# Gathering the second expert's rows ahead of its weights, with shorter index arithmetic, in a three-stage kernel

## The chip, the cores and the metric

The kernel runs on one core of one Trainium2 chip. The metric is the device time of one execution in microseconds (us). A core has TensorE (matmuls; PE in the profile, PEld for its weight loads), VectorE (DVE), ScalarE (ACT), GpSimd (POOL) and SyncE (SP), which work side by side and wait for each other by semaphores, and 16 DMA engines that are shared by all queues.

## The reference

Three stages in a chain. `B, H, S` are 4, 8, 576; the mixture has 2304 tokens of 512 values, 8 experts and room for 288 tokens in each.

```python
def reference(q, k, v, w_gate, w1, w2, w_in, w_out):
    x = windowed_attention(q, k, v)            # window 64
    x = x.transpose(0, 2, 1, 3).reshape(2304, 512)
    x = moe(x, w_gate, w1, w2)
    h = x @ w_in                               # 512 -> 2048
    return np.maximum(0.01 * h, h) @ w_out     # 2048 -> 512

def moe(x, w_gate, w1, w2):
    logits = x @ w_gate
    for idx in np.argsort(-logits.flatten()):
        tok, e = idx // 8, idx % 8
        if assigned[tok] >= 0 or counts[e] >= 288:
            continue
        assigned[tok] = e
        counts[e] += 1
    for e in range(8):
        mask = assigned == e
        out[mask] = np.maximum(x[mask] @ w1[e], 0.0) @ w2[e]
    return out
```

## The kernel before

Attention runs first and writes x to a DRAM tile `xd`. Then comes the routing, which is solved in 8 phases: each phase finds the next expert that fills up, with its 288 tokens. A phase (`Router.phase`) does 6 threshold rounds. In each round VectorE compares every token's best logit with a row of thresholds (`ge`), TensorE counts by expert (18 small matmuls `rp`), VectorE marks the thresholds that fill an expert (`sat`), one more matmul turns the marks into the threshold's bits (`pow`), and VectorE reduces them (`ns`). After the rounds VectorE works out which expert it is (`eidx`), each token's place in its list (`loc`) and in which third of 96 places that lies (`i1` for the second or third, `i2` for the third, `ind` for the three indicators). `rhs` holds the indicators times the token's chunk and partition number; a one-hot of the place in its third (`OB`, the tile `r_ob`) is multiplied with it in 18 matmuls, and a last small matmul with the constant `comb` gives the token numbers `ids`, 96 by 3. `gather_x` then has POOL issue three indirect DMAs that fetch 96 rows of x each (`xg`), and one that writes the ids, 1.1 KB, to a DRAM list `idl`. `xtrans` transposes a gathered third on TensorE (`xtp`), ScalarE copies it to `xT` (index 0, the high part) and VectorE subtracts to get the low part (index 1).

Experts and feed-forward blocks alternate: e0, e1, m0, e2, e3, m1, e4, e5, m2, e6, e7, m3, m4. An expert has 8 steps: `hstep` multiplies `xT` with a 512 KB block of weights (`raw`, `load_raw`) into `h` and applies relu (`hh`); `ystep` multiplies `hh` with the block's other half into four accumulators `ya`. From e1 on the weights are split (`split`) into a high part, copied by ScalarE, and a low part, subtracted by VectorE, and every product takes three matmuls; e0 uses its weights as they are, in fp32. At the end of an expert ScalarE copies the accumulators to `Y` and VectorE subtracts the low part. A feed-forward block has 16 steps (`h`, the leaky relu, `oa`) over up to 512 tokens, with weights that `Convert` has unpacked in pieces (`cv_in`, `cv_r`, `res`) on ScalarE and VectorE.

Every engine executes in the order in which the program emits. Up to e0 the order is written out: phase 0 is finished first (`R.finish(0, ...)`), with Convert pieces put in as fillers wherever a phase yields with a count above 0, and phase 1 runs in the gaps of e0. In the later part `RouteDriver.tick`, called between matmuls, decides from modelled engine clocks (`Clocks`, a cost for each instruction) whether a piece of the next routing phase, a waiting relu or a Convert piece is emitted next. At the end of e0, `run` finishes phase 1, gathers for e1, splits e1's first weights and transposes. All instructions that pass through `Clocks` carry the line 1019 of its recording helper in the profile, so operations are told apart by their tiles. PSUM buffers of tag `h` hold both first products and some of the transposes, two at a time.

Weights have five `raw` buffers. Step i asks for the blocks of steps i+1 to i+5 on SP's queue; the first time for an expert, the issuing engine loads `eidx` into a register (L658).

## Time and profile before

| | us |
|---|---|
| median of 3 runs | 862.91 |
| lowest and highest | 862.24 and 867.38 |
| profiled execution | 869.94 |
| span of its trace | 868.3 |

The mean granted clock of TensorE over the span is 0.968 of full speed. A row of the timeline gives the start in us from the span's start, the busy time, the engine, the tiles (`out<-in`), shapes, how many instructions were merged (x), and in brackets how long the engine was idle before and what released it. In the windows, PEclk is the granted clock of TensorE as a share of full speed.

### The profile page before, as it was taken

Reading aid. Unit: us, or ns where it says so; the run is one execution under the profiler, and the core shown is the slowest. Engines: PE = TensorE matmul, PEld = TensorE weight load, DVE = VectorE, ACT = ScalarE, POOL = GpSimd, SP = SyncE. Lnnn points to the kernel's source line nnn. Section 1 sums busy time; section 2 is a strip of 40 time slices with the busy share of each in tenths; the row PEclk is TensorE's granted clock in tenths of the full one; section 3 lists DMA queues with packets and bytes.
Section 4 is the critical chain, followed back from the end, with each engine's and each line's share of the span. In section 5 each row is a group of like instructions: output and inputs, shape, how many; then the busy total and the mean of one; then the engine's idle time right before and its main releaser. Section 6 shows DMA issues by size and latency. Waiting matters only on the chain.

```text
span 868.3 us, 15427 instructions
## 1 busy us (share of the span) xinstructions
PE 799.8 (92%) x5876; PEld 658.7 (76%) x5877; DVE 493.3 (57%) x1404; ACT 315.8 (36%) x707; POOL 130.8 (15%) x155
## 2 busy tenths in 40 slices
PE   6998972896999989999999998999999999999996
PEld 4666652575977867999777788997888998888895
DVE  3799988555776786988657587313223322222332
ACT  3677742203324663452111133532223452222221
POOL 2111101201001000300200005540002680000200
PEclk9999985898999999999999998999999999999999
DMA  9999823837104885574423237582343645222652
GB/s 267 312 306 280 265 89 133 180 116 153 44 1 148 292 314 171 188 132 132 141 71 117 102 101 179 145 212 76 121 146 99 178 165 194 97 96 100 242 194 97
DMA packets 43017, 138.78 MB, mean 160 GB/s; under 512 B 5696, under 2 KB 6336, under 8 KB 42944
## 3 DMA queue, kind: packets, MB, share of 16 engines
q1 hardware_dynamic: 38688, 126.34, 47.8%
q0 software_dynamic: 3680, 10.51, 4.0%
q8 instruction: 46, 0.75, 0.4%
q10 hardware_dynamic: 576, 0.95, 0.3%
q14 instruction: 27, 0.22, 0.1%
HBM read 117.85 MB, written 19.93 MB: 159 GB/s over the span
## 4 chain that ended last, share of the span: by engine, by line
PE 52%; DVE 5%; issue 4%; DMA 3%; ACT 2%; POOL 1%; POOLq 0%; SPq 0%; DVEq 0%; ACTq 0%
PE h L1019 25%; PE oa L1019 17%; PE ya L1019 7%; PE rp L1019 2%; DMA raw<-in_w_dram 2%; DMA cv_in<-in_wio_dram 1%; DVE w L1019 1%; DVE r_ob L1019 1%; DVE h L1019 1%; ACT cv_r L1019 1%; DVE hh L1019 1%; PE xtp L1019 1%; ACT cv_in L1019 0%; POOL w L1019 0%; DVE cv_r L1019 0%
## 5 line engine op out<-in xcount | busy, mean ns | idle before, releaser
L1019 PE MATMUL h<-Y,w 128*128 128x512 f32 (+1 forms) x600 | 139.4, 378 | 3.3 <-DVE hh L1019 3.3
L1019 PE MATMUL oa<-w,hh 128*128 128x512 f32 x540 | 133.6, 393 | 0.0
L1019 DVE SCALAR_TENSOR_TENSOR h<-h,tg 128x512 f32<-128x512 f32 (+1 forms) x80 | 51.5, 644 | 133.1 <-ACT tg L1019 131.1
L1019 PEld LDWEIGHTS h<-Y,w 128*128 128x128 f32 x600 | 105.0, 190 | 24.4 <-DVE hh L1019 3.5
L1019 ACT COPY tg<-h 128x512 f32<-128x512 f32 (+1 forms) x80 | 43.5, 544 | 219.9 <-PE h L1019 219.9
L1019 PEld LDWEIGHTS oa<-w,hh 128*128 128x128 f32 x540 | 99.8, 188 | 21.5 <-DVE hh L1019 0.3
L1019 PE MATMUL h<-xT,w 128*128 128x288 f32 x672 | 105.4, 305 | 0.9 <-ACT xT L1019 0.6
L1019 PE MATMUL ya<-hh,w 128*128 128x288 f32 x672 | 102.4, 300 | 0.4 <-issue 0.4
L1019 PEld LDWEIGHTS h<-xT,w 128*128 128x128 f32 x672 | 95.7, 194 | 2.2 <-ACT xT L1019 0.9
L1019 PEld LDWEIGHTS ya<-hh,w 128*128 128x128 f32 x672 | 93.1, 190 | 1.1 <-issue 0.7
L1019 PE MATMUL oa<-res,hh 128*128 128x512 f32 x324 | 82.2, 397 | 3.6 <-ACT hh L1019 2.9
L1019 PE MATMUL h<-Y,res 128*128 128x512 f32 (+1 forms) x360 | 84.4, 377 | 1.1 <-ACT Y L1019 1.1
L1019 ACT ACTIVATE hh<-h 128x288 fp32r<-128x288 f32 (+1 forms) x64 | 26.3, 410 | 136.9 <-PE h L1019 125.2
L1019 PEld LDWEIGHTS oa<-res,hh 128*128 128x128 f32 x324 | 59.2, 188 | 17.7 <-ACT hh L1019 4.2
L1019 PEld LDWEIGHTS h<-Y,res 128*128 128x128 f32 x360 | 62.2, 188 | 13.8 <-ACT Y L1019 1.6
L1019 DVE TENSOR_TENSOR hh<-h,hh 128x512 fp32r<-128x512 f32 (+1 forms) x80 | 50.9, 636 | 35.2 <-ACT hh L1019 34.0
L1019 POOL TENSOR_TENSOR w<-raw,w 128x512 fp32r<-128x512 f32 x41 | 51.8, 1292 | 116.9 <-ACT w L1019 114.0
L1019 POOL DMA_INDIRECT out_dram<-ot,sidx x18 | 18.9, 1052 | 330.2 <-DVE ot L1019 224.9
L1019 ACT CAST hh<-h 128x512 fp32r<-128x512 f32 (+1 forms) x80 | 43.5, 544 | 65.5 <-DVE h L1019 64.2
L1019 ACT CAST w<-raw 128x512 fp32r<-128x512 f32 x112 | 63.9, 618 | 7.7 <-DMA raw<-in_w_dram 7.7
L1019 DVE SCALAR_TENSOR_TENSOR hh<-h,hh 128x288 fp32r<-128x288 f32 x56 | 25.4, 454 | 65.6 <-ACT hh L1019 61.2
L1019 DVE TENSOR_TENSOR w<-raw,w 128x512 fp32r<-128x512 f32 x71 | 47.5, 706 | 4.5 <-ACT w L1019 2.9
(156 smaller groups left out, 961.6 us busy)
## 6 DMA issues: line engine op xcount, KB each, us to landing
w<-wsp SPq DMA_DIRECT2D x80, 512.0 KB, 3.7
raw<-in_w_dram SPq DMA_DIRECT2D x61, 512.0 KB, 5.4
cv_in<-in_wio_dram SPq DMA_DIRECT2D x32, 512.0 KB, 6.3
wsp<-w SPq DMA_DIRECT2D x20, 512.0 KB, 3.2
aq<-in_q_dram SPq DMA_DIRECT2D x12, 384.0 KB
avt<-in_vt_dram SPq DMA_DIRECT2D x12, 384.0 KB, 8.0
xd<-ax SPq DMA_DIRECT2D x18, 256.0 KB, 4.0
ak<-in_k_dram SPq DMA_DIRECT2D x8, 512.0 KB
```

The costliest lines, as they stand in the source:

```text
L1019: return f(*a, **kw)
```

## The change

1. The indicators are cumulative: `rhs` is one persistent tile whose first column is filled once in `start`, and the other two columns are made from `i1` and `i2` directly. `comb` takes the differences. The three `ind` operations of each phase go.
2. After the `pow` matmul a phase yields with 0 fillers instead of 1.
3. e0's first product of step 0 is done in thirds of 96 columns, each right behind its transpose.
4. At the end of e0 only the weights of e1's steps 0 and 1 (sequence steps 8 and 9) are requested before the gathers. Step 10's are requested on ScalarE's queue, those of 11 and 12 on POOL's, behind the gathers and the write of `idl`.
5. e0's four low parts of `Y` are subtracted after the transposes of e1.
6. `xtp` of the first two thirds of e2, and of the second third of e4 and e6, takes the PSUM tag `xt` (one buffer) instead of `h`.
7. `LEAD`, one modelled cost and two rules of `tick` in phase 1 change, which moves Convert pieces.

```diff
-    f['comb'][:6] = np.concatenate([128 * np.eye(3), np.eye(3)])
+    d = np.eye(3) - np.eye(3, k=-1)
+    f['comb'][:6] = np.concatenate([128 * d, d])
...
+        v.tensor_copy(self.rhs[:, :, 0, 0], cf['cid'])
+        v.tensor_copy(self.rhs[:, :, 1, 0], cf['pid'].to_broadcast([128, NT]))
...
                 nc.tensor.matmul(pa, self.pow2[r][:J], sat[:J], start=True, stop=True)
-                yield 'v', 1
+                yield 'v', 0
...
-        g.tensor_scalar(out=ind[:, :, 0], in0=i1, scalar1=-1.0, scalar2=1.0, op0=ALU.mult, op1=ALU.add)
-        g.tensor_tensor(out=ind[:, :, 1], in0=i1, in1=i2, op=ALU.subtract)
-        g.tensor_copy(ind[:, :, 2], i2)
-        yield 'd', 0
-        rhs = t([128, NT, 2, 3], BF, "rhs", ph)
-        g.tensor_tensor(out=rhs[:, :, 0], in0=ind, in1=b3(cf['cid'], NT, 3), op=ALU.mult)
-        g.tensor_scalar(out=rhs[:, :, 1], in0=ind, scalar1=cf['pid'], scalar2=None, op0=ALU.mult)
+
+        g.tensor_tensor(out=self.rhs[:, :, 0, 1:], in0=i12, in1=b3(cf['cid'], NT, 2), op=ALU.mult)
+        g.tensor_scalar(out=self.rhs[:, :, 1, 1:], in0=i12, scalar1=cf['pid'], scalar2=None, op0=ALU.mult)
...
-FORCE, LEAD = 4, 10
+FORCE, LEAD = 4, 12
...
-        if a == 1 or n + a == 2:
+        if n < 2 and n + a == 2 or a == 1 and (n % 2 or n == 0):
             pt = self.pp.tile([128, 4, 96], F32, tag="h", name=f"xtp{n}_{a}")
...
         if kind == "e" and n == 0:
+            if p == 0:
+
+                for k in range(4):
+                    nc.tensor.matmul(ph[:, 96 * hi:96 * hi + 96], w[:, 128 * k:128 * k + 128], self.xT[n][0][:, hi, k].bitcast(F32), start=(k == 0), stop=(k == 3), skip_group_check=True)
+                return
...
-                for low in range(2):
+                def rows(low, acc=self.acc):
...
+                rows(0)
+                if n:
+                    rows(1)
+                else:
+
+                    self.lows = lambda: rows(1)
...
         for a in range(3):
             self.xtrans(0, a)
+            self.hprod(0, a)
...
-            for j in range(i + 1, i + 6):
+
+            for j in range(i + 1, i + 6 if self.ng > 1 else min(i + 6, first[1] + 2)):
                 self.load_raw(j)
             if yfirst:
                 self.ystep(i)
                 if i + 1 == first[1]:
 
-                    R.finish(1, lambda: [self.load_raw(j) for j in range(i + 1, i + 6)])
+                    R.finish(1, lambda: [self.load_raw(j) for j in range(i + 1, i + 3)])
                     self.gather_x(1)
                     self.ng = 2
+                    self.load_raw(i + 3, nc.scalar)
+                    for j in range(i + 4, i + 6):
+                        self.load_raw(j, nc.gpsimd)
                     for j in range(i + 1, i + 3):
                         self.split(j, 0)
                     self.split(i + 1, 1)
                     for a in range(3):
                         self.xtrans(1, a)
+                    self.lows()
...
-            return max(n[0] * (1.75 if ins[0].dtype == F32 and ins[1].dtype == F32 and ins[1].shape != ins[0].shape else 0.447) + 1, 25)
+            return max(n[0] * (1.68 if ins[0].dtype == F32 and ins[1].dtype == F32 and ins[1].shape != ins[0].shape else 0.447) + 1, 25)
...
-            elif self.conv.done < self.goal and dve - t <= self.BACK and self.conv.piece():
+            elif self.conv.done < self.goal and not one and dve - t <= self.BACK and self.conv.piece():
...
-            elif dve - t > self.CBACK or not self.conv.piece():
+            elif dve - t > (-self.SPARE if one else self.CBACK) or not self.conv.piece():
                 return
```

The first place is TensorE at the start of e0. `xtp_0` to `xtp_2` are the transposes, `xg_0` the gathered rows of e0, the first `h` is the first product. Before:

```order
L1019 MATMUL warm<-cbt 128x512
L1019 LDWEIGHTS cbt
L1019 MATMUL warm<-cbt 128x512
L1019 MATMUL xtp_0_2518<-cft,xg_0_2448 128x96 x4
L1019 MATMUL xtp_1_2524<-cft,xg_0_2450 128x96 x4
L1019 MATMUL xtp_2_2530<-cft,xg_0_2452 128x96 x4
L1019 MATMUL h_2540<-xT_0_2516,raw_2391 128x288
```

And after:

```order
L1037 MATMUL warm<-cbt 128x512
L1037 MATMUL xtp_0_2499<-cft,xg_0_2429 128x96 x4
L1037 MATMUL h_2505<-xT_0_2497,raw_2377 128x96 x4
L1037 MATMUL xtp_1_2510<-cft,xg_0_2431 128x96 x4
L1037 MATMUL h_2505<-xT_0_2497,raw_2377 128x96 x4
L1037 MATMUL xtp_2_2520<-cft,xg_0_2433 128x96 x4
L1037 MATMUL h_2505<-xT_0_2497,raw_2377 128x96 x4
L1037 MATMUL h_2536<-xT_0_2497,raw_2379 128x288
```

Each third of the product now stands behind its own transpose, and the round of phase 1 that stood behind the first two matmuls of step 0 (`rp`, from `r_ge`) stands behind the first matmuls of step 1.

The second place is VectorE at the end of phase 1, where the ids of e1 are made. `w_8` and `w_9` are low parts of e1's first weights. Before:

```order
L1019 TENSOR_TENSOR r_rhs_2886<-r_ind_2871,cft 128x18x3
L1019 TENSOR_SCALAR r_rhs_2886<-r_ind_2871,cft 128x18x3
L1019 TENSOR_TENSOR r_ob_2889<-r_lb_2877,cbt 128x864 x2
L1019 TENSOR_TENSOR w_9_2912<-raw_2906,w_9_2912 128x512
L1019 TENSOR_TENSOR w_8_2915<-raw_2904,w_8_2915 128x512
L1019 COPY r_ip_2940<-rp_2890 6x96
L1019 CAST r_ids_2948<-rp_2943 96x3
L1019 SCALAR_TENSOR_TENSOR r_uw<-r_cw_2848,r_mi_2852,r_uw 128x8
```

And after:

```order
L1037 TENSOR_TENSOR r_rhs<-r_i_1_2881,cft 128x18x2
L1037 TENSOR_SCALAR r_rhs<-r_i_1_2881,cft 128x18x2
L1037 TENSOR_TENSOR r_ob_2905<-r_lb_2885,cbt 128x864 x2
L1037 COPY r_ip_2933<-rp_2906 6x96
L1037 CAST r_ids_2939<-rp_2936 96x3
L1037 SCALAR_TENSOR_TENSOR r_uw<-r_cw_2856,r_mi_2860,r_uw 128x8
L1037 TENSOR_SCALAR r_ac_2865<-r_ac_2865 128x18
```

The three `ind` operations are gone, and the two weight subtractions no longer stand between the one-hot and `r_ip`; they follow some 15 rows further down, ahead of the low parts of `xT`.

The third place is ScalarE and POOL between e0 and e1. `Y` from `ya` are e0's results, `xT` from `xtp` the transposed rows of e1, `w` from `raw` the high parts of e1's weights. ScalarE before:

```order
L1019 CAST Y_0_0_2094<-ya_0_2600 128x288
L1019 CAST Y_1_0_2096<-ya_1_2601 128x288
L1019 CAST Y_2_0_2098<-ya_2_2602 128x288
L1019 CAST Y_3_0_2100<-ya_3_2603 128x288
L1019 CAST w_8_2994<-raw_2904 128x512
L1019 CAST xT_0_2997<-xtp_0_2999 128x384
L1019 CAST xT_0_2997<-xtp_1_3006 128x384
L1019 CAST xT_0_2997<-xtp_2_3013 128x384
L1019 CAST w_10_3020<-raw_2908 128x512
L1019 CAST w_9_3023<-raw_2906 128x512
L1019 ACTIVATE hh_3060<-h_3026 128x288
L1019 CAST w_11_3065<-raw_2910 128x512
```

ScalarE after, from the last of e0's results on (`raw_2983` belongs to step 10, `raw_2994` to step 11):

```order
L1037 CAST Y_3_0_2103<-ya_3_2591 128x288
L658 TENSOR_LOAD r_eidx_2870
L658 ISA x2
L1037 ISA
L1037 DMA raw_2983<-in_w_dram 128x1024
L1037 CAST w_8_2998<-raw_2897 128x512
L1037 CAST w_9_3001<-raw_2899 128x512
L1037 CAST w_8_3004<-raw_2897 128x512
L1037 CAST xT_0_3007<-xtp_0_3009 128x384
L1037 CAST xT_0_3007<-xtp_1_3016 128x384
L1037 CAST xT_0_3007<-xtp_2_3023 128x384
L1037 CAST w_10_3034<-raw_2983 128x512
```

POOL before, from the gathers of e1 to those of e2:

```order
L1019 DMA xg_1_2987<-xd,r_ids_2948 96x512
L1019 DMA xg_1_2989<-xd,r_ids_2948 96x512
L1019 DMA xg_1_2991<-xd,r_ids_2948 96x512
L1019 DMA idl<-r_ids_2948 96x3x1
L1019 DMA sidx_3593<-idl 128x4x1
L1019 DMA xg_2_3694<-xd,r_ids_3652 96x512
```

And POOL after:

```order
L1037 DMA xg_1_2967<-xd,r_ids_2939 96x512
L1037 DMA xg_1_2969<-xd,r_ids_2939 96x512
L1037 DMA xg_1_2971<-xd,r_ids_2939 96x512
L1037 DMA idl<-r_ids_2939 96x3x1
L658 TENSOR_LOAD r_eidx_2870
L658 ISA x2
L1037 ISA
L1037 DMA raw_2994<-in_w_dram 128x1024
L1037 ISA
L1037 DMA raw_2996<-in_w_dram 128x1024
L1037 DMA sidx_3572<-idl 128x4x1
```

On ScalarE the load of `eidx` and the request for step 10's weights now stand behind e0's results, with three copies of weights behind them and ahead of `xT`. On POOL the requests for steps 11 and 12 stand behind the three gathers and the write of `idl`.

## Rows read from the trace of the kernel before

**Rows 1.** Page: the chain that ended last, shares of the span by engine.
```profile
PE 52%; DVE 5%; issue 4%; DMA 3%; ACT 2%; POOL 1%; POOLq 0%; SPq 0%; DVEq 0%; ACTq 0%
```

**Rows 2.** Timeline, one round of phase 0: start, us, engine, operation [idle <-releaser].
```profile
133.51 0.67 DVE L1019 TENSOR_TENSOR res<-cv_r,res 128x512 fp32r<-128x512 f32 x1
133.63 0.16 PE L1019 MATMUL rp<-r_sat,pow 31*128 31x8 bf16 x1 [0.55 <-DVE r_sat L1019]
134.11 0.15 DVE L1019 TENSOR_REDUCE r_ns<-rp 128x1 int32<-128x8 f32 x1
```

**Rows 3.** Timeline, the same step of a phase 1 round.
```profile
178.13 0.17 PE L1019 MATMUL rp<-r_sat,pow 31*128 31x8 bf16 x1
...
178.34 0.17 DVE L1019 TENSOR_REDUCE r_ns<-rp 128x1 int32<-128x8 f32 x1 [1.12 <-PE rp L1019]
```

**Rows 4.** Timeline, POOL from the indicators of phase 0 to the gathers.
```profile
145.93 0.22 POOL L1019 TENSOR_SCALAR r_ind<-r_i 128x18 f32<-128x18 f32 x1 [31.13 <-DVE r_i L1019]
...
155.65 1.02 POOL L1019 DMA_INDIRECT xg<-xd,r_ids  x1 [0.30 <-issue]
```

**Rows 5.** Timeline, VectorE at the one-hot of phase 0.
```profile
146.27 2.03 DVE L1019 TENSOR_TENSOR r_ob<-r_lb,cbt 128x864 bf16<-128x864 bf16 x2
```

**Rows 6.** Timeline, TensorE from the ids of phase 0 into expert 0.
```profile
149.37 1.60 PE L1019 MATMUL rp<-r_ob,r_rhs 128*6 128x96 bf16 x18 [7.37 <-POOL r_rhs L1019]
...
156.37 0.55 PE L1019 MATMUL xtp<-cft,xg 96*128 96x96 f32 x4 [0.62 <-DMA xg<-xd,r_ids]
...
158.95 0.55 PE L1019 MATMUL xtp<-cft,xg 96*128 96x96 f32 x4 [0.81 <-DMA xg<-xd,r_ids]
160.07 0.75 PE L1019 MATMUL h<-xT,raw 128*128 128x288 f32 x2 [0.57 <-ACT xT L1019]
```

**Rows 7.** Windows: us, busy time by engine (x), PEclk, DMA share, GB/s.
```profile
162.00:165.00 3.00, 3.00 (x8) 1.80 (x7) 1.37 (x7) 0.00 (x0) 0.00 (x0) 0.50 1.10 45
209.00:217.00 8.00, 7.21 (x45) 6.36 (x46) 3.40 (x8) 2.95 (x6) 0.15 (x1) 0.57 0.94 62
325.00:329.00 4.00, 4.00 (x28) 2.96 (x27) 1.47 (x4) 0.00 (x0) 0.00 (x0) 0.57 0.68 268
```

**Rows 8.** Timeline, TensorE between expert 0 and expert 1.
```profile
199.46 0.33 PE L1019 MATMUL rp<-cft,r_ip 6*96 6x3 f32 x2 [2.10 <-DVE r_ip L1019]
199.71 4.15 PE L1019 MATMUL ya<-hh,raw 128*128 128x288 f32 x16
...
209.22 0.75 PE L1019 MATMUL xtp<-cft,xg 96*128 96x96 f32 x4 [1.17 <-DVE xT L1019]
210.54 1.09 PE L1019 MATMUL h<-xT,w 128*128 128x288 f32 x3 [0.57 <-ACT xT L1019]
```

**Rows 9.** Timeline, ScalarE there.
```profile
197.30 1.14 ACT L1019 CAST w<-raw 128x512 fp32r<-128x512 f32 x2 [4.81 <-DMA raw<-in_w_dram]
...
202.44 1.85 ACT L1019 CAST Y<-ya 128x288 fp32r<-128x288 f32 x4 [3.70 <-PE ya L1019]
```

**Rows 10.** Timeline, VectorE there.
```profile
197.95 1.29 DVE L1019 TENSOR_TENSOR w<-raw,w 128x512 fp32r<-128x512 f32 x2 [2.36 <-ACT w L1019]
```

**Rows 11.** Timeline, POOL there.
```profile
202.80 0.91 POOL L1019 DMA_INDIRECT xg<-xd,r_ids  x1 [0.30 <-issue]
...
216.85 0.80 POOL L1019 DMA_DIRECT2D sidx<-idl  x1 [12.39 <-DMA idl<-r_ids]
```

**Rows 12.** DMA issues of 203 to 206 us: KB each, us to landing.
```profile
raw<-in_w_dram SPq DMA_DIRECT2D x1, 512.0 KB, 12.5
```

**Rows 13.** Timeline, VectorE and TensorE at the start of m0's second products.
```profile
251.17 0.69 DVE L1019 SCALAR_TENSOR_TENSOR h<-h,tg 128x512 f32<-128x512 f32 x1
...
252.54 0.50 PE L1019 MATMUL oa<-res,hh 128*128 128x512 f32 x1 [1.67 <-ACT hh L1019]
```

**Rows 14.** Timeline, VectorE and TensorE near the end of m0.
```profile
323.96 0.68 DVE L1019 TENSOR_TENSOR hh<-h,hh 128x512 fp32r<-128x512 f32 x1
...
324.70 0.50 PE L1019 MATMUL h<-Y,w 128*128 128x512 f32 x1 [3.33 <-DVE hh L1019]
```

More of the change, by code (lines that the diff above doesn't have):

```diff
@@ L279, in __init__ @@
         self.rem0 = pool.tile([128, 8], F32, name="r_rem0")
+        self.rhs = pool.tile([128, NT, 2, 3], BF, name="r_rhs")
     def start(self):
@@ L464, in phase @@
         TS(out=loc, in0=self.slotg, scalar1=iw, scalar2=None, op0=ALU.add)
-        ind = t([128, NT, 3], F32, "ind", ph)
         yield 'd', 0
-        i1, i2 = t([128, NT], F32, "i1", ph), t([128, NT], F32, "i2", ph)
+        i12 = t([128, NT, 2], F32, "i12", ph)
+        i1, i2 = i12[:, :, 0], i12[:, :, 1]
         TS(out=i1, in0=loc, scalar1=95.5, scalar2=None, op0=ALU.is_gt)
@@ L487, in phase @@
             for c in range(lo if ph == 0 else 0, hi if ph == 0 or lo else 0):
-                nc.tensor.matmul(pi, rhs[:, c].rearrange("p a b -> p (a b)"), OB[:, c], start=(c == 0), stop=(c == NT - 1))
+                nc.tensor.matmul(pi, self.rhs[:, c].rearrange("p a b -> p (a b)"), OB[:, c], start=(c == 0), stop=(c == NT - 1))
         yield 'v', 1
@@ L672, in split @@
             return
-        if kind == "e" and i not in self.raw:
+        if kind == "e" and (i not in self.raw or n >= self.ng):
             return
@@ L725, in hprod @@
         self.hdone[i] = hi
-        if lo == 0:
+        if i not in self.ph:
             self.ph[i] = self.pp.tile([128, 512], F32, tag="h", name=f"h{i}")
@@ L757, in hstep @@
         N = 288 if kind == "e" else self.mslots(n)[1]
-        self.hprod(i, 12)
+        if i:
+            self.hprod(i, 12)
         ph = self.ph[i]
@@ L826, in ystep @@
                             hi, lo = (y[d][pos // 512][:, pos % 512:pos % 512 + c] for y in self.Y)
-                            src = self.acc[d][:, s:s + c]
+                            src = acc[d][:, s:s + c]
                             if low:
@@ L1025 @@
     BACK, FWD, CBACK, PBACK, SLACK, HOLD = 300, 50, 0, 4000, 100, 200
+    SPARE = 700
     def __init__(self, nc, router, conv):
@@ L1054, in tick @@
             t, dve = self.nc.at["tensor"], self.nc.at["vector"]
+            one = self.ph == 1
             if self.jobs and self.jobs[0][1] <= max(t, dve):
```

## Prediction

> **What bounds the kernel now.** I read the page first: the chain that ended last lies on TensorE for 52% of the span, with VectorE next at 5% [rows 1]. So what counts is TensorE's idle time and the places where its clock is low, and I went through its timeline for idle times. After e1 has started they are few: the largest are 3.33 us near the end of m0 and 1.67 us at its start [rows 13, 14]. The rest of what can be won lies between attention and e1, where there are two serial stretches: phase 0 of the routing (122 to 152 us), in which TensorE waits for VectorE and POOL, and the gap between e0 and e1 (197 to 210.5 us). TensorE's queue is nearly full afterwards, so what is saved there should reach the end.
>
> The windows show the second price of an idle stretch. After the sparse start of e0 the granted clock is 0.50 for 162 to 165 us, after the gap before e1 it is 0.57 over 209 to 217 us, after the m0 stall 0.57 over 325 to 329 us [rows 7]; these are means of the levels 1.2 and 2.4 GHz. Against full clock that is 3 x 0.5 = 1.5 us, 8 x 0.43 = 3.4 us and 4 x 0.43 = 1.7 us.
>
> **Phase 0, the filler after `pow`.** In a round the `pow` matmul ends at 133.63 + 0.16 = 133.79 us, but `ns` starts at 134.11, because the filler `res` (133.51, 0.67 us) is in front of it [rows 2]. In phase 1, where no filler stands there, `ns` starts at 178.34, 0.04 us after the matmul's end at 178.30 [rows 3]. So 0.32 - 0.04 = 0.28 us goes in each of 6 rounds: 1.7 us. The six pieces are not saved: they are done in phase 1 instead, where VectorE has room. If they come too late, m0 waits for its weights.
>
> **Phase 0, the indicators.** POOL's five operations run from 145.93 us, and the 18 matmuls start at 149.37 after POOL [rows 4, 6]. Two operations are left, without the three in front: from 0.44 us (twice the 0.22 us of the first) to two fifths of the stretch of 3.44 us, 1.4 us. Both are done by 147.4 us, so the one-hot on VectorE is what comes last: it ends at 146.27 + 2.03 = 148.30 us [rows 5]. The matmuls start on its first half and take 1.60 us, so they end some 0.1 us behind either POOL's or VectorE's last input plus a half: I take 149.2 to 149.4 instead of 150.97. Gain 1.6 to 1.8 us, taken as 1.6. Phase 0 gives 3.3 us in all (2.5 to 3.6).
>
> **e0's first product in thirds.** The last gather is issued at 155.65 and its transpose starts at 158.95, 3.30 us later [rows 4, 6]; h starts at 160.07. An fp32 matmul of this size is two rows of 0.26 us (sixteen took 4.15 [rows 8]), so h's four are 2.1 us of work and could be through at 162.1; the routing round that stands between them moves behind and costs the same there. With thirds only the last one is left behind the last transpose, but the links stand in order: three times a transpose of 0.55 us, 0.57 us for the copy (the idle time ahead of h) and 0.7 us for a third, 5.5 us from the first transpose at 156.37 [rows 6], which is 161.8. So 0 us (-0.4 to +0.7). TensorE is less idle there, and the low clock at 162 us may be shorter: I take 0.8 of the 1.5 us (0 to 1.5).
>
> **Between e0 and e1, up to the gathers.** Before, `comb` starts at 199.46 after 2.10 us of idle time [rows 8]. What came last is VectorE's `r_ip`, which stood behind two subtractions of weights (197.95, 1.29 us), these behind two copies on ScalarE at 197.30 that had waited for the raw weights (4.81 us of idle time, released by DMA) [rows 9, 10]. In the change these four stand behind `ids`, and two of the `ya` matmuls come ahead of `comb` on TensorE. h ends at 199.46 - 2.10 = 197.36; two matmuls of 0.52 us behind it give a start at 198.4, 1.1 us earlier (0.5 to 1.6); call it T.
>
> **From the gathers to h of e1.** Before, the third gather is issued at 202.80, 3.34 us after `comb` [rows 8, 11]. The last transpose comes at 209.22 and h at 210.54 = `comb` + 11.08 [rows 8]. A gather without other traffic took 3.30 us in phase 0, so the third is there at T + 6.7. Then ScalarE decides: the four copies of `Y` (1.85 us from 202.44 [rows 9]) begin behind the first `ya` accumulators and end at T + 3.8 to 4.8 by their place behind `comb` before (2.98 + 1.85), less the two matmuls that have moved; the load of `eidx` and a DMA issue stand next (an issue on POOL has 1.02 us [rows 4]; I take 1 to 1.6), then three copies of weights, 3 x 0.57 = 1.7 us [rows 9], and only then the copies of `xT`; on VectorE three subtractions of 0.65 us [rows 10] stand ahead. I put h at T + 9.0 to 9.5, so 1.6 to 2.1 us better than before. With the 1.1 us this is 2.7 to 3.2 us. TensorE has nearly the same sparse stretch in front of it, so I leave the 3.4 us of clock as they are.
>
> **The weights of steps 10 to 12.** This is the edit that costs. They were requested on SP ahead of or beside the gathers; now step 10's goes out at about T + 5.1 and those of 11 and 12 at about T + 6.5 on POOL's queue behind the write of `idl`. That write is 1.1 KB in pieces of 4 bytes, and the POOL instruction that needed it waited until 216.85, 12.39 us [rows 11]; a raw block requested beside it took 12.5 us to land [rows 12], and in 209 to 217 us the DMA engines were 94% busy at 62 GB/s [rows 7]. So I let raw 10 land 5 to 12.5 us after its issue, at T + 10 to 17.6, and raw 11 and 12 8.5 to 14, at T + 15 to 20.5. ScalarE is in order: the copies of step 10's weights stand ahead of the first relu of e1, without which the first `ya` can't run; that one is due at about T + 16: h at T + 9.3, 12 matmuls of 0.36 us at the low clock (three took 1.09 us [rows 8]) and step 9's 12 at half of that, 6.5 us. Copies and relu take 1.5 us, so it is late by 0 to 3 us; the same holds for step 11. I take 1.5 us of loss for both (0 to 5). Net of the gap: 2.8 - 1.5 = 1.3 us (-2.2 to +6, the latter with the clock).
>
> The Trainium skill speaks against this edit: its page "DMA: Bandwidth & Descriptors", section "Issuing engines are not separate DMA queues", says that requests from SP, ScalarE and GpSimd run on the same 16 engines and interleave, so that another issuing engine saves only the issue time. By that rule the moved requests gain nothing from their new queues, and the loss would be at its upper bound, 5 us; rows 12 agree as far as they go, since the slow block on SP's queue ran beside a write from POOL's.
>
> **The low parts of `Y`** (four subtractions) move behind `xT` on VectorE. The first that needs them is m0, behind all of e1: 0 us, and what VectorE no longer has in front of `xT` is counted above.
>
> **m0.** At its start `oa` waits 1.67 us for `hh`, whose leaky relu on VectorE stands at 251.17 behind a burst of routing operations [rows 13]. In the new order only part of the burst stands ahead of it. Half of the wait, 0.8 us (0 to 1.67). Near its end TensorE waits 3.33 us after e2's first transpose, since the next h needs the buffer that `hh` frees at 323.96 + 0.68 [rows 14]. With the transpose in another buffer h doesn't need that one; but the new order puts a routing round ahead, whose comparison is late on VectorE too. I take 1.2 us (0 to 5.0, which is the stall and its 1.7 us of clock).
>
> **Convert pieces and costs.** The modelled costs move pieces, and the number done by the end of phase 1 and in m0 stays: 0 us (-1 to +1).
>
> **Sum.** 3.3 + 0 + 0.8 + 1.3 + 0 + 0.8 + 1.2 + 0 = 7.4 us. The profiled execution has 868.3 us of span and 1.64 us around it, 869.94 us; 7.4 less is 862.5. That execution is 7.03 us above the median of 862.91, but its waits are those of the program, so I take the difference over: 862.91 - 7.4 = 855.5 us, 0.86% less. About 1% (8.6 us) is what a measurement of this kernel tells from no change.
>
> **Rivals.** (A) The gap closes better: raw 10 to 12 arrive in time, the clock before e1 or e0 doesn't fall as long, and the m0 stall goes. For it: without traffic a gather landed in 3.3 us, so the slow write may finish earlier too. Against: the same write was slow at 209 to 217 us with one block beside it. Then 3.3 + 1.5 + 6 + 1.7 + 3 = 15.5 at most; I take 12, 851 us. (B) The late weights take the wait's place: each of raw 10, 11 and 12 needs the 12.5 us of rows 12 after its issue, and one behind another on POOL's ring (T + 17.6, 22, 27). ScalarE stands at each copy with a relu behind it, TensorE idles 3 + 4 + 4 us and pays the 3.4 us of clock once more: 14.4 us lost against 2.8 + 3.3 + 0.8 + 2 gained, so 868 us, 5 us slower than before; 2 us more per block would take it over 1%. It decides if the weights of step 11 land after T + 19. For it: rows 11 and 12; against: before, blocks issued on POOL behind the first `idl` write serve e0's steps 3 and 4, and no stall of TensorE shows there. (C) The gap doesn't do what it says: ScalarE's chain fully takes the place of the late gathers, and in m0 VectorE is late anyway. Then only phase 0 and `comb` are left: 3.3 + 1.1 + 0.3 = 4.7, 858.2 us.
>
> **How the numbers follow.** The forecast with its own spread (852 to 859, within it some under 854.3) 0.45; A 0.23; C 0.20; B 0.12. The range 849 to 863 leaves out the better end of A and most of B. Faster by over 1%: A and a quarter of the forecast, 0.34. Slower by over 1% (above 871.5): a third of B, 0.05. Within: 0.61.
>
> **What would show it.** Right: `ns` 0.05 us behind `pow` in phase 0, ids about 3.3 us earlier; `comb` without idle time in front, gathers that land 3.3 us after issue, h of e1 9 to 9.5 us after `comb`; in m0 shorter waits at both places. Wrong: idle time of TensorE before the first three `ya` of e1, with ScalarE's copies of raw 10 to 12 waiting for DMA; a low clock that lasts longer after 209 us; VectorE with Convert pieces that TensorE waits for in m0.

## The result, and the profile after

| | before | after |
|---|---|---|
| median of 7 runs, us | 864.49 | 872.68 |
| lowest and highest, us | 862.16 and 867.38 | 870.18 and 874.51 |
| span of the profiled execution, us | 868.3 | 872.5 |

The change makes the kernel slower: the ratio is 1.0091, 95% interval 1.0067 to 1.0116. That is 8.2 us more, against a forecast of 7.4 us less.

The chain that ended last, shares of the span after the change:

```profile
PE 70%; DVE 17%; DMA 6%; ACT 3%; issue 2%; SPq 1%; POOL 0%; POOLq 0%; DVEq 0%; ACTq 0%
```

It can't be set beside [rows 1]: the shares there add up to 67%, because that chain is followed back only to 284.38 us, while the one above reaches back to the start. So [rows 1] says nothing of the stretch from 122 to 210 us, in which most of the change works; that TensorE sets the pace there has to be read from the timelines.

Starts of the same instructions in the two timelines show where the time goes. The last column is what each stretch adds, from unrounded starts.

| start of | before | after | difference | added |
|---|---|---|---|---|
| `comb` of phase 0 | 151.31 | 147.14 | -4.2 | -4.2 |
| first transpose of e0 | 156.37 | 154.18 | -2.2 | +2.0 |
| relu of e0's step 1 | 167.03 | 169.31 | +2.3 | +4.5 |
| `comb` of phase 1 | 199.46 | 206.78 | +7.3 | +5.0 |
| h of e1 | 210.54 | 216.02 | +5.5 | -1.8 |
| first `ya` of e1 | 217.34 | 221.20 | +3.9 | -1.6 |
| h of m0 | 245.01 | 251.93 | +6.9 | +3.1 |
| h of e2 | 347.62 | 354.36 | +6.7 | -0.2 |
| h of m1 | 410.81 | 419.31 | +8.5 | +1.8 |

The timeline of after for phase 0 and the start of e0, on TensorE, VectorE, POOL, ScalarE and SP:

```profile
131.90 0.16 PE L1037 MATMUL rp<-r_sat,pow 31*128 31x8 bf16 x1 [0.55 <-DVE r_sat L1037]
...
132.10 0.17 DVE L1037 TENSOR_REDUCE r_ns<-rp 128x1 int32<-128x8 f32 x1 [0.25 <-PE rp L1037]
...
143.47 0.25 POOL L1037 TENSOR_TENSOR r_rhs<-r_i,cft 128x36 bf16<-128x36 f32 x1 [29.64 <-DVE r_i L1037]
...
143.71 0.38 POOL L1037 TENSOR_SCALAR r_rhs<-r_i,cft 128x36 bf16<-128x36 f32 x1
...
143.57 0.90 SPq L660 DMA_DIRECT2D raw<-in_w_dram  x2
...
145.05 1.75 PE L1037 MATMUL rp<-r_ob,r_rhs 128*6 128x96 bf16 x18 [5.54 <-DVE r_ob L1037]
...
147.71 0.62 ACT L1037 CAST res<-cv_r 128x512 fp32r<-128x512 f32 x1 [9.49 <-DVE cv_r L1037]
...
148.69 1.14 POOL L1037 DMA_INDIRECT xg<-xd,r_ids  x1 [4.61 <-DVE r_rem L1037]
...
148.98 0.36 ACTq L1037 DMA_DIRECT2D raw<-in_w_dram  x1
...
154.18 0.55 PE L1037 MATMUL xtp<-cft,xg 96*128 96x96 f32 x4 [1.91 <-DMA xg<-xd,r_ids]
...
155.29 1.95 PE L1037 MATMUL h<-xT,raw 128*128 128x96 f32 x8 [0.57 <-ACT xT L1037]
...
158.45 2.02 PE L1037 MATMUL h<-xT,raw 128*128 128x96 f32 x8 [0.57 <-ACT xT L1037]
...
161.69 3.04 PE L1037 MATMUL h<-xT,raw 128*128 128x96 f32 x10 [0.57 <-ACT xT L1037]
```

`ns` starts 0.04 us behind `pow`, as in [rows 3] and not as in [rows 2]. POOL has two operations of 0.25 and 0.38 us, and the 18 matmuls now wait for VectorE's one-hot and not for POOL ([rows 4, 6]). Then the gain runs away. The gather issued at 148.69 us is there only at 154.18, 5.5 us later instead of 3.5. Before, SP's request for e0's weights and the first gather stood further apart:

```profile
145.98 0.93 SPq L660 DMA_DIRECT2D raw<-in_w_dram  x2
...
152.88 1.15 POOL L1019 DMA_INDIRECT xg<-xd,r_ids  x1 [3.56 <-issue]
```

The gather now comes 5.1 us behind that request instead of 6.9. ScalarE's request for a block of weights, which had gone out at 145.97 before, now stands behind a Convert copy that waited 9.49 us, and leaves at 148.98, beside the gathers. And a third of the product takes 1.95 to 2.02 us for eight rows (one matmul each), where [rows 6] had let me expect 0.7.

The stall in e0, on TensorE, VectorE, ScalarE and SP (in this order, from the effect back to the cause):

```profile
179.43 0.64 PE L1037 MATMUL rp<-r_oh,r_ge 128*31 128x8 bf16 x18 [3.15 <-DVE r_ge L1037]
...
177.60 0.69 DVE L1037 SCALAR_TENSOR_TENSOR cv_r<-cv_r,cv_in 128x512 int32<-128x512 int32 x1 [4.54 <-ACT cv_in L1037]
...
176.37 0.66 ACT L1037 ACTIVATE cv_r<-cv_in 128x512 f32<-128x512 f32 x1 [6.64 <-DMA cv_in<-in_wio_dram]
...
171.25 0.33 SPq L660 DMA_DIRECT2D raw<-in_w_dram  x1
...
171.67 0.86 SPq L560 DMA_DIRECT2D cv_in<-in_wio_dram  x2
```

TensorE idles 3.15 us for `r_ge`; VectorE's row before it stood behind a Convert piece that waited 4.54 us for ScalarE, ScalarE waited 6.64 us for the block `cv_in`, and SP had issued that block only at 171.67, behind a raw block that had to wait for a buffer.

The clock, in windows of after (columns as in [rows 7]):

```profile
158.00:162.00 4.00, 2.98 (x13) 2.69 (x14) 0.00 (x0) 0.88 (x2) 0.00 (x0) 0.50 0.91 33
...
162.00:166.00 4.00, 4.00 (x29) 3.23 (x29) 0.18 (x2) 1.51 (x3) 0.00 (x0) 0.50 0.59 85
...
180.00:184.00 4.00, 4.00 (x12) 2.51 (x10) 2.38 (x9) 0.00 (x0) 0.00 (x0) 0.50 0.48 190
...
216.00:220.00 4.00, 3.98 (x16) 3.98 (x17) 3.41 (x8) 1.42 (x3) 0.00 (x0) 0.50 0.99 81
...
328.00:332.00 4.00, 2.01 (x15) 1.90 (x16) 2.63 (x5) 1.08 (x3) 0.00 (x0) 0.69 0.92 326
332.00:336.00 4.00, 4.00 (x10) 3.04 (x10) 1.88 (x4) 1.01 (x2) 0.00 (x0) 0.50 0.55 219
```

It is 0.50, the level of 1.2 GHz, all through the thirds, again behind the stall, before e1's first `ya`, and behind the stall near the end of m0. Between e0 and e1, and in m0, on TensorE and ScalarE, against [rows 8, 9, 13, 14]:

```profile
206.78 0.33 PE L1037 MATMUL rp<-cft,r_ip 6*96 6x3 f32 x2
...
214.55 0.90 PE L1037 MATMUL xtp<-cft,xg 96*128 96x96 f32 x4 [1.87 <-DVE xT L1037]
...
216.02 5.34 PE L1037 MATMUL h<-xT,w 128*128 128x288 f32 x24 [0.57 <-ACT xT L1037]
...
223.19 1.14 ACT L1037 CAST w<-raw 128x512 fp32r<-128x512 f32 x2 [3.41 <-DMA raw<-in_w_dram]
...
228.08 0.45 PE L1037 MATMUL rp<-r_oh,r_ge 128*63 128x8 bf16 x9 [1.41 <-DVE r_ge L1037]
...
324.41 3.00 PE L1037 MATMUL oa<-w,hh 128*128 128x512 f32 x12 [0.92 <-ACT hh L1037]
...
329.99 0.64 PE L1037 MATMUL rp<-r_oh,r_ge 128*63 128x8 bf16 x9 [2.19 <-DVE r_ge L1037]
```

`comb` has no idle time in front of it any more, and h of e1 starts 9.24 us behind it instead of 11.08. But ScalarE's copy of step 11's weights waits 3.41 us for its DMA, VectorE's low part of them stands ahead of `r_ge`, and TensorE waits 1.41 us for that. In the answers on DMA issues, the two blocks on POOL's queue take 14.4 us to land in e0 and 12.1 us in e1, a block on SP beside the latter 13.5. Step 10's block, on ScalarE's queue, takes only 3.9:

```profile
raw<-in_w_dram POOLq DMA_DIRECT2D x2, 512.0 KB, 14.4
...
raw<-in_w_dram POOLq DMA_DIRECT2D x2, 512.0 KB, 12.1
...
raw<-in_w_dram SPq DMA_DIRECT2D x1, 512.0 KB, 13.5
...
raw<-in_w_dram ACTq DMA_DIRECT2D x1, 512.0 KB, 3.9
```

That block left together with the write of the ids, and not behind it:

```profile
211.03 0.74 POOL L1037 DMA_DIRECT2D idl<-r_ids  x1
...
211.07 0.36 ACTq L1037 DMA_DIRECT2D raw<-in_w_dram  x1
```

From m1 to the end the difference falls from 8.5 us to 4.2. Most of that is a low clock in before from 536 us on that after does not have:

```profile
536.00:540.00 4.00, 3.57 (x25) 3.07 (x22) 2.43 (x6) 1.08 (x3) 0.08 (x1) 0.63 1.22 74
...
540.00:544.00 4.00, 4.00 (x19) 4.00 (x18) 0.00 (x0) 0.35 (x1) 2.44 (x2) 0.52 0.56 33
```

That is 3.4 us. Ahead of it TensorE waits 1.32 and 0.43 us for VectorE's one-hot in before, and 0.35 us in after. Whether the median executions have it isn't shown; if they don't, it is why the spans differ by 4.2 us where the medians differ by 8.2.

### The profile page after: what moved, and what is told of

It is laid out like the page before. It is cut to its first block, busy times and chain, and to the rows that moved or that the text cites. A ratio compares the mean times of both kernels' runs of the same rounds, so it can differ in the third digit from the quotient of the medians.

```text
span 872.5 us, 15447 instructions
## 1 busy us (share of the span) xinstructions
PE 807.0 (92%) x5893; PEld 663.5 (76%) x5893; DVE 493.6 (57%) x1387; ACT 316.3 (36%) x707; POOL 126.7 (15%) x152
## 4 chain that ended last, share of the span: by engine, by line
PE 70%; DVE 17%; DMA 6%; ACT 3%; issue 2%; SPq 1%; POOL 0%; POOLq 0%; DVEq 0%; ACTq 0%
PE h L1037 31%; PE oa L1037 20%; PE ya L1037 10%; PE rp L1037 4%; DMA cv_in<-in_wio_dram 3%; PE as L137 2%; DVE w L1037 2%; DVE r_ob L1037 1%; DMA raw<-in_w_dram 1%; DVE amx L139 1%; DVE h L1037 1%; PE xtp L1037 1%; DVE hh L1037 1%; DVE cv_r L1037 1%; DVE ax L180 1%
## 5 line engine op out<-in xcount | busy, mean ns | idle before, releaser
L1037 PE MATMUL oa<-w,hh 128*128 128x512 f32 x540 | 136.0, 395 | 0.9 <-ACT hh L1037 0.9
L1037 PE MATMUL ya<-hh,w 128*128 128x288 f32 x672 | 100.4, 296 | 0.2 <-ACT hh L1037 0.2
L1037 POOL TENSOR_TENSOR w<-raw,w 128x512 fp32r<-128x512 f32 x39 | 49.2, 1291 | 115.1 <-ACT w L1037 115.1
```

The lines of the kernel that those rows point to most:

```text
L1037: return f(*a, **kw)
```

## Experiments

Three theories for the loss: S, starved Convert pieces hold VectorE and so TensorE in e0; T, the thirds cost TensorE time at a low clock; and W, the weights of steps 10 to 12 come late, either because the write of the ids jams the DMA engines (J) or because ScalarE's and POOL's queues are slow (Q). Ratios are to the kernel before, run beside each, with 95% intervals; the changed kernel has 1.0091. The median of the kernel before lay between 864.49 and 868.69 us in the five groups of runs, so times of different groups are compared by their ratios alone.

**The parts undone one at a time.** The filler back:

```diff
-                yield 'v', 0
+                yield 'v', 1
```

> The changed kernel with the filler behind the pow matmul put back (one Convert piece in each of phase 0's 6 rounds). Theory S (starved pieces: with fewer pieces done in phase 0, fewer cv_in loads stand ahead of the fifth raw block on SP's queue, which waits for a buffer; a piece in e0 then waits for its cv_in and VectorE's routing round behind it holds TensorE for 3.15 us at 179 us, with 3 us of low clock): the wait of TensorE for r_ge in e0 falls from 3.2 to under 0.5 us, phase 0 is 1.7 us longer, in all 3 to 5 us less than the changed kernel, 868 to 870 us. Theory W (late weights of steps 10 to 12 are the loss): the stall in e0 may go, but the total is 1.7 us more, about 874 us. Theory T (thirds at a low clock): about the same as the changed kernel.

Measured 1.0055 (1.0035 to 1.0076). TensorE has no wait for `r_ge` in e0 over 0.4 us. This is what S expected, but the interval touches that of the changed kernel; the run by itself further down settles it.

The whole first product back:

```diff
             self.xtrans(0, a)
-            self.hprod(0, a)
...
-        if i:
-            self.hprod(i, 12)
+        self.hprod(i, 12)
```

> The changed kernel with e0's first product in one piece again. Theory T (a third of 96 columns costs nearly 1 us of TensorE at full clock and 2 at the low one, since its eight rows of weights have to be loaded for each third; the three thirds end 9.6 us after the first transpose, and the clock stays low until 168 us): step 1's relu of e0 comes 3 to 5 us earlier against ids, and the total is 3 to 5 us below the changed kernel, 868 to 870 us. Theory S alone: the product's place has no effect on the stall at 179 us, total less by under 1 us, unless the order of the cv_in loads changes with it. Theory W: no change, 872 to 873 us.

Measured 1.0037 (1.0018 to 1.0055). TensorE's timeline there:

```profile
155.73 1.32 PE L1030 MATMUL h<-xT,raw 128*128 128x288 f32 x2 [0.60 <-ACT xT L1030]
...
158.04 2.29 PE L1030 MATMUL h<-xT,raw 128*128 128x288 f32 x4
...
160.37 3.53 PE L1030 MATMUL h<-xT,raw 128*128 128x288 f32 x10
```

The product of step 0 is done before the relu at 161.74, and step 1's relu comes at 163.94, 18.0 us behind `comb` where the changed kernel has 22.2: 4.2 us for T. At the low clock a row of 288 columns takes 0.57 us (2.29 for 4), so eight are 4.6 us; three thirds of eight rows at 0.25 us are 6.0 us. The rest is the clock: it is low here too, but only from 156 to 162 us (0.97 in the two us behind), where the changed kernel has 0.50 until 168. All 17 profiles agree: in the six kernels with thirds step 1's relu starts 14.4 to 15.3 us behind the first transpose, in the eleven with the whole product 10.3 to 12.0. The tick between the matmuls also puts a `cv_in` block more ahead of the fifth raw block, and the stall in e0 is gone. But the first `ya` of e1 waits 5.45 us for its relu.

All five blocks requested on SP again:

```diff
-            for j in range(i + 1, i + 6 if self.ng > 1 else min(i + 6, first[1] + 2)):
+            for j in range(i + 1, i + 6):
...
-                    R.finish(1, lambda: [self.load_raw(j) for j in range(i + 1, i + 3)])
+                    R.finish(1, lambda: [self.load_raw(j) for j in range(i + 1, i + 6)])
...
-                    self.load_raw(i + 3, nc.scalar)
-                    for j in range(i + 4, i + 6):
-                        self.load_raw(j, nc.gpsimd)
```

> The changed kernel with the weights of steps 8 to 12 requested on SP at eidx, ahead of the gathers, as before. Theory W: the wait of e1's first three second products for weights goes (3.1 us lost between the first ya of e1 and m0), h of e1 comes later against comb by about 2 us; in all 1 us less to 1 us more than the changed kernel. Theories S and T: stall in e0 and low clock as in the changed kernel, so 871 to 874 us.

Measured 1.0121 (1.0092 to 1.0149), at least not better: the transposes wait 1.52, 1.92 and 4.25 us for gathers that run beside the weights, and h of e1 starts 14.0 us behind `comb`. Gathering first does what it is for.

Filler and whole product both back:

> The changed kernel with both the filler and the whole first product back. Theories S and T together: both losses go, about 7 us less than the changed kernel and 1 to 3 us more or less than the kernel before, 862 to 867 us. Theory W: still 3 us behind the kernel before for the late weights, 866 to 870 us.

Measured 1.0029 (1.0008 to 1.0049): the stall and the loss to thirds are both gone, and what is left is a wait of 5.72 us at e1's first `ya`, for late weights (shown below).

**S by itself.** One more `cv_in` block staged, so that it stands ahead of the raw block that waits:

```diff
-        while len(self.conv.st) < 3:
+        while len(self.conv.st) < 4:
```

> The changed kernel with one more cv_in block requested before e0 (four staged instead of three), so that it stands ahead of the fifth raw block on SP's queue; nothing else. Theory S: the wait of 3.15 us for r_ge in e0 goes, and the low clock behind it (3 us); total 3 to 6 us below the changed kernel, ratio to before 1.002 to 1.006. If the stall in e0 was only a sign of something else (thirds at a low clock), it stays and the ratio is 1.008 to 1.010.

Measured 1.0036 (1.0015 to 1.0058). The stall is gone, and with it more than half of the loss. S is shown: the place of one `cv_in` block on SP's queue decides it.

**Why the weights are late.** The writes of ids moved behind the last weights in the program, on POOL's queue: first in the kernel with filler and product back, then in the changed kernel, then in the one before:

```diff
+            if i == first[1] + 5:
+                self.put_ids(0)
+                self.put_ids(1)
```

> Filler and whole first product back, and the two writes of 4-byte ids (for e0 and e1) moved from behind their gathers to step 5 of e1, when its last weights have been asked for. Theory J (the write of 288 pieces of 4 bytes jams the DMA engines for some 8 to 10 us, whatever queue the others are on): step 10's weights land about 5 us after their issue instead of 15, the wait of 5.7 us before e1's first ya goes and with it 3 us of low clock; e0's steps 3 and 4 get their weights in 5 to 7 us. Total 8 to 10 us below the kernel with filler and product back, 858 to 862 us. Theory Q (blocks on POOL's queue are slow, and keep ScalarE's queue waiting, whether or not the ids are written): the landing stays over 10 us, total 866 to 870 us.

> The changed kernel with the two writes of ids moved to step 5 of e1, nothing else. Theory J: weights of e0's steps 3 and 4 and of e1's steps 10 to 12 land in 5 to 7 us, the 3 us lost between the first ya of e1 and m0 go; the stall of 3.15 us at 179 us in e0 stays or shrinks a little, since the cv_in blocks stand behind the fifth raw block; total 3 to 6 us below the changed kernel. Theory Q: within 1 us of the changed kernel.

> The kernel before with the two writes of ids moved to step 5 of e1. Theory J: the raw block that took 12.5 us beside the write lands in 5 to 6 us; TensorE did not wait for it, so the total moves by 0 to 2 us only (an earlier end of low DMA rate in e0). Theory Q: no change at all in any landing time.

Measured 0.9986 (0.9959 to 1.0014), 1.0076 (1.0049 to 1.0104) and 1.0037 (1.0011 to 1.0064). The edit did only half of what it should: POOL had nothing to wait for and issued both writes at once, behind e1's gathers and its own requests for weights (in the last of the three at 202.40 us), so they ran there as before, twice as large. The third is slower than the kernel before, though nothing on TensorE's path was meant to change there; no run explains it. In e0 the write is away, though. The DMA rate just behind the gathers, in windows of the kernel before and then of the same kernel with the writes moved (columns as in [rows 7]):

```profile
161.00:163.00 2.00, 2.00 (x20) 1.49 (x17) 0.77 (x2) 0.14 (x1) 0.00 (x0) 0.65 0.83 37
```

```profile
159.00:161.00 2.00, 2.00 (x22) 1.46 (x23) 0.66 (x2) 0.94 (x2) 0.00 (x0) 0.80 0.99 371
```

The engines are busy in both, at 83% and 99%, but move 37 GB/s beside the write and 371 GB/s without it. Both windows begin 2.4 us behind the end of POOL's requests for weights. So J holds in e0. For e1 it was left open, and the next runs settle it. Steps 10 to 12 on SP's queue, in the kernel with filler and product back:

```diff
-                    self.load_raw(i + 3, nc.scalar)
-                    for j in range(i + 4, i + 6):
-                        self.load_raw(j, nc.gpsimd)
+                    for j in range(i + 3, i + 6):
+                        self.load_raw(j)
```

> Filler and whole first product back, and the weights of steps 10 to 12 requested on SP's queue behind the gathers, with the write of the ids in its place. Theory J: the first of them still lands only after the write, 8 to 12 us after its issue, the wait before e1's first ya shrinks to 2 to 4 us because SP issues earlier than ScalarE did; total 1 to 3 us below the kernel with filler and product back, 866 to 868 us. Theory Q: landing in 5 us, no wait before the first ya; total 6 to 9 us below, 860 to 863 us.

Measured 0.9911 (0.9881 to 0.9941), the gain that Q expected and more than J did, but not by Q's mechanism: the blocks requested beside the write still took 10.2 us (median). SP waits neither for ScalarE's copies nor for the gathers, so step 10's block left at 196.07 us, ahead of the gathers and of the write, and only the later ones ran into it.

The writes on SP's queue, which comes to them only behind its last weights, and the queues of steps 10 to 12 as in the change:

```diff
+            if i == first[1] + 5:
+                self.put_ids(0, nc.sync)
+                self.put_ids(1, nc.sync)
```

> Filler and whole first product back, weights of steps 10 to 12 on ScalarE's and POOL's queues as in the change, and the two writes of ids on SP's queue behind the request for e1's last weights, so that they can no longer run beside steps 10 to 12. Theory J (the 4-byte write jams the engines): step 10's block lands 4 to 6 us after its issue instead of 15, the wait of 5.7 us before e1's first ya goes, total 6 to 9 us below the kernel with filler and product back, 860 to 863 us. Theory Q (it is the queues of ScalarE and POOL): landing over 10 us, total 866 to 869 us.

Measured 0.9950 (0.9931 to 0.9969), against 1.0029 without this edit. The first `ya` of e1 and the landing of step 10's block on ScalarE's queue, with the write beside it and then without:

```profile
220.51 1.81 PE L1030 MATMUL ya<-hh,w 128*128 128x288 f32 x6 [5.72 <-ACT hh L1030]
...
raw<-in_w_dram ACTq DMA_DIRECT2D x1, 512.0 KB, 15.0
```

```profile
212.20 1.86 PE L1037 MATMUL ya<-hh,w 128*128 128x288 f32 x12
...
raw<-in_w_dram ACTq DMA_DIRECT2D x1, 512.0 KB, 7.7
```

15.0 us become 7.7, and the wait of 5.72 us is gone, on the same queues. J is the cause of this wait. With the write beside it, the block had left 2.5 us behind the write:

```profile
201.50 0.75 POOL L1030 DMA_DIRECT2D idl<-r_ids  x1
...
203.99 0.36 ACTq L1030 DMA_DIRECT2D raw<-in_w_dram  x1
```

In the changed kernel it left 0.04 us behind it and landed after 3.9 us, so there the jam reached step 11's block and not step 10's.

Both edits together, and the first of the two without the filler:

> As the run with steps 10 to 12 on SP's queue (858.8 us), with the two writes of ids on SP behind e1's last weights. Theory J: step 11's and 12's blocks no longer take 10 us, e0's DMA rate has no gap after its gathers; TensorE waited little for them there, so 0 to 3 us less, 856 to 859 us. Theory Q: no change in e1; 0 to 1 us.

> As the run with steps 10 to 12 on SP's queue, but without the filler behind pow (as in the change). Theory S: with the whole product another cv_in block already stands ahead of the fifth raw block, so there is no stall in e0, and phase 0 is 1.7 us shorter: 0.5 to 2 us less than 858.8 us. If a piece of Convert still waits in e0: 2 to 4 us more.

Measured 0.9902 (0.9875 to 0.9929) and 0.9911 (0.9887 to 0.9934). Without the stall the filler is worth nothing either way: the second has the ratio that the same queues gave with the filler (0.9911). Its `comb` of phase 0 comes 3.8 us earlier than there (145.74 and 149.56), but the first transpose only 2.7 us (153.71 and 156.40).

**The indicators alone**, in the kernel before (the first part of the diff above):

> The kernel before with the cumulative indicators alone. By the prediction's term the 18 matmuls of phase 0 end 1.6 to 1.8 us earlier. If the gathers then land as early (3.3 us after issue), 1.5 us less than before, ratio 0.998. If the gathers meet the weights requested at eidx (in the change the first gather took 5.4 us instead of 3.5), the gain is given back: ratio 0.999 to 1.001.

Measured 0.9994 (0.9975 to 1.0014), which can't tell the two apart. The timeline can, for the place: the first transpose starts 6.8 us behind `comb` (147.18 and 153.97) instead of 5.1, so 1.7 us are given back to slower gathers. ScalarE's request for weights leaves at 143.52 there, well ahead of the gathers, so its slip in the changed kernel isn't needed for this. In all 17 profiles the first transpose starts 10.3 to 11.7 us behind SP's request for e0's weights, whether the first gather stands 5.1 or 6.9 us behind that request.

**The thirds by themselves**, put into the best kernel so far:

> As the run with steps 10 to 12 on SP and the ids written late (ratio 0.990), with e0's first product in thirds again: the thirds alone. Theory T: three thirds take TensorE 2 us each at the low clock and keep it sparse, 2 to 5 us more, ratio 0.993 to 0.996. If thirds only looked bad beside the jam (the transposes also waited for gathers), within 1 us, ratio 0.990 to 0.991.

Measured 1.0080 (1.0050 to 1.0109), 1.8% above 0.9902, more than any theory asked. The relu of step 1 on ScalarE, with thirds and without:

```profile
170.35 0.41 ACT L1043 ACTIVATE hh<-h 128x288 f32<-128x288 f32 x1 [3.74 <-PE h L1043]
```

```profile
164.87 0.41 ACT L1036 ACTIVATE hh<-h 128x288 f32<-128x288 f32 x1 [1.64 <-PE h L1036]
```

From `comb` (148.90 and 147.74) these are 21.5 and 17.1 us: 4.3 us, as T has it. The other 11 us come later. As I read it they are not the thirds themselves: a third has no tick between its matmuls, so the routing and all that the modelled clocks place after it is emitted in another order. `comb` of phase 1 then comes 32.6 us behind that relu instead of 28.9, the transposes of e1 wait 3.95 us for gathers, and a low clock at 540 to 552 us comes on top. How much of it each of these takes stays open.

**The favoured form of each part** (whole product, no filler, SP's queue, late ids):

> Whole first product, no filler behind pow, steps 10 to 12 on SP, ids written late: what the runs so far favour of each part. By the two neighbours (0.9911 without the late ids, 0.9902 with the filler): 0 to 2 us less than the better of them, ratio 0.987 to 0.990. If the gathers of e0 meet the weights requested at eidx, the earlier ids bring nothing and the ratio stays at 0.990.

Measured 0.9934 (0.9908 to 0.9961): no better than 0.9902 with the filler, whose interval it overlaps. Several versions beat both kernels; the lowest ratio is that one's, 855.63 us where the kernel before had 864.94.

## Why the prediction was wrong

The forecast was 15.6 us too low (-7.4 against +8.2). By the stretches of the table its terms are -3.3, 0, -0.8, -1.1, -1.7, 0, +1.5, -2.0 and 0; measured less forecast is -0.9, +2.0, +5.3, +6.1, -0.1, -1.6, +1.6, +1.8 and +1.8 us, 16 us up to m1 in the two profiled executions. The two largest, in e0, decide the sign. The first reading was wrong as well: the 52% of [rows 1] belong to a chain that begins at 284 us, though no term rests on them.

**Right.** The filler (0.28 us per round) and the indicators, as far as `comb`: from the one-hot's start to the end of the 18 matmuls it takes 3.0 us (143.78 to 146.80) instead of 4.7, 1.7 us as said. `comb` of phase 1 has no wait in front, and h of e1 comes at T + 9.24, inside 9.0 to 9.5. The loss for late weights was put at 1.5 us, 0 to 5. From h of e1 to m0 it is 1.4: the -1.6 and +3.1 of the table belong together, since a routing round that stood ahead of the first `ya` now stands behind it. TensorE idles 1.8 us there (0.16, 0.21 and 1.41). The size is right and the late weights are the cause, but the way is another: step 10's block was in time, and it is step 11's that holds VectorE's `r_ge`, not a relu. In m0 the wait of 1.67 us for `hh` at the start is gone; 0.30 us is left there, for the routing.

**Wrong, the largest: "e0's first product in thirds. So 0 us", and the 0.8 us of clock on top.** I took 0.7 us for a third, from rows at full clock, and took the columns to set the time. The clock is at its low level when the thirds run, and the sparse chain of thirds keeps it there until 168 us; and a row of 96 columns takes 0.25 us at that level, where a third of the 0.57 us of 288 columns would be 0.19. So 4.2 to 4.5 us are lost, where I expected 0.8 won: 5.0 to 5.3 us.

**Wrong: "Convert pieces and costs ... 0 us (-1 to +1)".** I counted the pieces done by the end of phase 1 and did not ask where their inputs stand on SP's queue. With six fewer in phase 0 the buffers of `cv_in` come free later, the next request falls behind a raw block that waits for its own buffer, and a piece without input holds VectorE's in-order queue. That is 3.15 us of stall and 3.4 us of low clock behind it (0.66, 0.50 and 0.98 in the windows of 4 us from 178 us on). The stretch adds 5.0 us where 1.1 less was forecast, 6.1 in all; one staged block more removes the stall.

**Wrong: that ids 3.3 us earlier bring the rows 3.3 us earlier.** I called the 3.30 us of a gather its time without other traffic; it was the price of the third one, 9.7 us behind SP's request for e0's weights. The rows come 10.3 to 11.7 us behind that request in every profile. So the 2.4 us by which the request itself came earlier reach the transpose (2.2 us), and the 1.8 us that the indicators won behind it are lost: 2.0 us of the 4.2 at `comb`. That the gathers share the DMA engines with these weights is the reading that fits; no run took the weights away.

**Wrong: m0's end, 1.2 us.** It still idles 0.92 and 2.19 us, 3.11 instead of 3.33, as VectorE's comparison is late there, and the low clock behind it costs 3.4 us (0.69, 0.50 and 0.96 in the windows of 4 us from 328 us on) instead of 1.7. With the gain at its start m0 comes out at -0.2 us, against -2.0.

**No term at all.** From h of e2 to h of m1 another 1.8 us are lost. TensorE waits 0.67 and 0.34 us for VectorE's one-hot and `r_ip` there, which it doesn't before; the cause of the rest stays open.

Rival B had the mechanism of the late weights, at 14 us a price that the changed kernel does not pay, because step 10's block leaves with the write and not behind it; with the filler and the whole product back it leaves behind it, and the wait shows in full (5.72 us). What I gave no rival at all, the thirds and the Convert pieces, is what decided the sign, and the range of 849 to 863 us was too low for it. The rule of the Trainium skill that I weighed ("DMA: Bandwidth & Descriptors", "Issuing engines are not separate DMA queues") is borne out: behind the write the blocks take 10.2 to 15.0 us on all three queues, and without it 7.7 us on ScalarE's, 6.2 on POOL's and 4.7 on SP's. The loss at its upper bound, 5 us, which I drew from it, did not come. The same page of the Trainium skill ("Specifications") puts line rate at 512 bytes and more and names a read-modify-write below; the runs show the jam that such writes make, but none shows what in it takes the time.

## What to carry to other kernels

Moving filler work later also moves the requests for its inputs; look where they then stand on an in-order DMA queue, and behind which wait. A tiny write in 4-byte pieces can hold up blocks of 512 KB that are requested behind it, so it belongs where nothing urgent is in flight. Indices that were ready earlier brought nothing here, where their gathers came in behind weights that had been requested ahead of them. Splitting a matmul by columns multiplies its weight loads (24 instead of 8 here; those of a third kept the loading busy for 1.71 to 1.78 of its 1.95 to 2.02 us), so price the pieces at the clock at which they will run.

## What was not expected of the hardware

Beside a write of 1.1 KB in 288 pieces the 16 DMA engines were 83% busy at 37 GB/s, and a 512 KB block that another queue requested 2.5 us behind such a write took 15.0 us instead of 7.7; one requested with it took 3.9. An fp32 matmul row of 96 columns took 0.25 us at the low clock, where one of 288 took 0.57: a third of the columns cost some 43% of the time. And nearly the same waits for the one-hot were followed by a low clock in one kernel and not in another: 1.13 and 0.43 us around 532 us with filler and product back and the writes moved on POOL's queue (0.58 from 532 to 536 us), 1.15 and 0.42 us around 526 us with steps 10 to 12 on SP's (1.00 throughout). So a low clock there in one profile and not in another is not by itself the mark of an edit.
